# Adding x off TensorE for 14 of 16 blocks of pairs, with PSUM copies shared anew and the steps reordered

## The chip, the cores and the metric

One core of a Trainium2 chip. The rounds of the experiments ran on four different chips, so kernels of different rounds are compared by their ratios to before, which ran in every round. The metric is device time in microseconds (us), the median of several executions; lower is better. The span that the profile shows (first to last instruction) is some 2 us shorter than that time. Executions have states: a few are slow (over 1.5% above the fastest of the same kernel) and are left out of ratios.

## The reference

Linear attention over 8 batches x 8 heads x 576 rows x 64, then a highway layer (512 wide) on its 4608 rows. H and T are the carry and the gate of the kernel.

```python
q_s = softmax(q, axis=-1); k_s = softmax(k, axis=2)         # written out in the reference
kv  = einsum('bhsd,bhse->bhde', k_s, v)
x   = einsum('bhsd,bhde->bhse', q_s, kv)  -> rows of 512
H = maximum(x @ w_h, 0); T = sigmoid(x @ w_t + b_t)
out = T * H + (1 - T) * x
```

## The kernel before

Everything is written as small steps, and one list, `order`, says in which order they are issued. Each engine works off its own part of that list strictly in order. So the list is the schedule. The steps that matter here:

```python
ld = pool("ld", 3)                       # three buffers each for q, k and v in float32
def load(b, which, parts=1): ...         # nc.sync.dma_start, one batch of q, k or v
def cast_v(b, a):                        # GpSimd: half a batch of v to float16
    nc.gpsimd.tensor_copy(o, i)
def q_scale_p(b, n0, n1):                # GpSimd: exp(q) times 1/sum
    nc.gpsimd.tensor_mul(e, e, r.broadcast_to(list(e.shape)))
turned = (6, 7)
def q_turn(b, n0, n1):                   # batches 6 and 7: q is transposed by DMA, queue of SyncE
    nc.sync.dma_start_transpose(out=qsD[b][...], in_=eq[b][:, n0:n1]...)

added = lambda g: ((0, 1), (0, 1, 2), (0, 1, 2), (0, 1, 2, 3))[g]   # g: pair of batches
def add_x(c, ob):                        # blended part g += x, off TensorE
    eng = nc.vector if (c, ob) == (B - 1, 3) else nc.gpsimd
    eng.tensor_add(gv(ob), gv(ob), xv(ob))
def turn_block(t, k_, xs, us):           # output: transpose by a matmul with the identity
    if xs is not None:
        mm(dst, xs, ident, True, False)  # x added in PSUM: one 128x128 matmul more
    mm(dst, us, ident, xs is None, True)
def out_copy(g, n, eng): ...             # output tile PSUM -> SBUF on ScalarE or VectorE; every 4th: store

order = [
    # ... cut: 470 steps; here only what goes to GpSimd and SyncE near the end, in order
    ("load", 7, "k"), ("q_scale_p", 6, 4, 9), ("q_turn", 6, 0, 4), ("cast_v", 6, 0),
    ("q_turn", 6, 4, 9), ("load", 7, "v"), ("cast_v", 6, 1), ("add_x", 4, 0), ...
    ("q_scale_p", 7, 0, 4), ("add_x", 5, 0), ("q_scale_p", 7, 4, 9),
    ("cast_v", 7, 1), ("cast_v", 7, 0), ("add_x", 5, 2), ("add_x", 5, 1), ...
]   # the two queues are each in true order; how they interleave is simplified
for name, *args in order:
    steps[name](*args)
```

A *unit* is a gate or a carry of one batch and one output block (128 of the 512 columns): four 128x512 matmuls. The *k-v product* of a batch is exp(k) times v, and x of a batch is its scaled q times that. A *scaling* is one call of `q_scale_p`; each batch has two. A *filler* is a clock-keeping matmul.

The softmax here doesn't subtract the row's maximum and nothing guards it: scores larger than these inputs give would overflow.

## Time and profile before

| before | value |
|---|---|
| time, median of 3 (range) | 125.06 us (124.79 to 125.07) |
| span of the profiled run, granted clock | 122.5 us, 0.999 |
| busy: PE, VectorE, ScalarE, GpSimd | 111.3, 95.9, 92.9, 79.8 us |
| first gate; x of batches 1, 3, 6, 7 | 21.8; 29.65, 53.05, 85.06, 95.18 us |
| last matmul needed, end | 118.35, 122.53 us |

TensorE's busy time is modelled and holds clock-keeping matmuls ("warm"), so 91% is not 91% of useful work. Better signposts are the moments at which x of a batch starts: each needs q, k and v of that batch through all engines. The prediction below shows the slices, the stretches and TensorE's waits of this kernel.

### The profile page before, as it was taken

The page shows a single profiled execution, that of the slowest core. Times are in us where ns is not written, and L with a number is a line of the kernel's source. Part 1 is how long each engine was busy: PE and PEld are TensorE (multiplying, and loading weights), DVE is VectorE, ACT ScalarE, POOL GpSimd, SP SyncE. Part 2 cuts the span into 40 slices and gives each one's busy share as a digit, 9 for nine tenths or more (in the row PEclk, how much of TensorE's full clock was granted, in tenths as well). Part 3 has the DMA queues.
Part 4 walks back from the last instruction along what each step waited for, and adds up shares of the span by engine and source line. Part 5 has one row for each costly group of instructions (what it writes and reads, how often), then busy time and mean ns, then how long its engine had stood idle before and what let it go on. Part 6 is the DMA issues. An engine that isn't in the chain of part 4 may idle for free.

```text
span 122.5 us, 3361 instructions
## 1 busy us (share of the span) xinstructions
PE 111.3 (91%) x1371; PEld 61.5 (50%) x1371; DVE 95.9 (78%) x179; ACT 92.9 (76%) x130; POOL 79.8 (65%) x75
## 2 busy tenths in 40 slices
PE   4998985998999998999997999997999999999960
PEld 1344543354336444745745464454456545599830
DVE  1079796579999999999979996898656379779960
ACT  4193737496979998789979999983986895588650
POOL 2000487952279989599899899996995307934620
PEclk9999999999999999999999999999999999999999
DMA  3999999999999999999999999999977500539995
GB/s 100 388 402 408 409 399 397 410 412 411 406 412 409 402 411 412 415 398 416 417 356 404 411 411 401 418 212 246 438 171 214 219 0 0 206 144 390 423 384 175
DMA packets 20583, 41.24 MB, mean 337 GB/s; under 512 B 5460, under 2 KB 5976, under 8 KB 19544
## 3 DMA queue, kind: packets, MB, share of 16 engines
q1 hardware_dynamic: 20568, 41.03, 89.0%
q8 instruction: 10, 0.16, 0.5%
q14 instruction: 5, 0.04, 0.1%
HBM read 30.41 MB, written 9.44 MB: 325 GB/s over the span
## 4 chain that ended last, share of the span: by engine, by line
DMA 51%; PE 28%; ACT 5%; POOL 5%; SPq 3%; DVE 3%; issue 2%; ACTq 0%; POOLq 0%
DMA q<-in_q_dram 24%; DMA k<-in_k_dram 12%; PE ph L64 11%; DMA w32h<-in_moe_w_h_dram 9%; PE pt L64 9%; DMA qsD<-eq 6%; PE nat L64 5%; ACT eq L174 4%; SPq L94 3%; POOL eq L254 3%; POOL g L424 2%; PE px L64 1%; DVE r L224 1%; ACT xT L357 1%; PE psk L64 1%
## 5 line engine op out<-in xcount | busy, mean ns | idle before, releaser
L64 PE MATMUL pt<-xT,w16t 128*128 128x512 f16 x128 | 32.9, 380 | 0.4 <-ACT xT L361 0.3
L254 POOL TENSOR_TENSOR eq<-eq,r 128x1024 f16<-128x1024 f16 (+2 forms) x16 | 29.9, 1876 | 4.7 <-DVE r L242 1.6
L64 PE MATMUL ph<-xT,w16h 128*128 128x512 f16 x128 | 32.5, 379 | 0.4 <-DVE dd L405 0.2
L424 POOL TENSOR_TENSOR g<-g,xT 128x512 f16<-128x512 f16 x23 | 26.0, 1154 | 7.1 <-DVE g L413 4.9
L392 ACT ACTIVATE pt<-pt,bt 128x512 f32<-128x512 f32 (+1 forms) x40 | 24.8, 632 | 6.2 <-PE pt L64 5.2
L413 DVE SCALAR_TENSOR_TENSOR g<-pt,dd 128x512 f16<-128x512 f32 (+1 forms) x40 | 24.9, 632 | 4.9 <-ACT pt L392 4.3
L405 DVE SCALAR_TENSOR_TENSOR dd<-xT,ph 128x512 f16<-128x512 f16 x32 | 21.1, 677 | 6.7 <-PE ph L64 6.6
L174 ACT ACTIVATE eq<-q 128x1152 f16<-128x1152 f32 x16 | 18.3, 1168 | 7.1 <-DMA q<-in_q_dram 7.1
L185 POOL CAST v<-v 128x1152 f16<-128x1152 f32 x12 | 13.7, 1154 | 13.2 <-DMA v<-in_v_dram 12.8
L64 PEld LDWEIGHTS <-w16h 128*128 128x128 f16 x160 | 14.5, 98 | 13.2 <-issue 1.6
L64 PEld LDWEIGHTS <-w16t 128*128 128x128 f16 x160 | 14.3, 98 | 12.7 <-issue 1.1
L224 DVE TENSOR_REDUCE r<-eq 128x18 f32<-128x1152 f16 x12 | 16.0, 1345 | 6.0 <-ACT eq L174 6.0
L464 ACT COPY o<-nat 128x512 f32<-128x512 f32 x28 | 16.8, 601 | 4.4 <-PE nat L64 3.5
L174 ACT ACTIVATE ek<-k 128x1152 f16<-128x1152 f32 x16 | 18.4, 1175 | 1.6 <-DMA k<-in_k_dram 1.5
L64 PE MATMUL warm<-wide,ident 128*128 128x512 f16 x53 | 15.1, 427 | 1.8 <-DVE wide L144 1.8
L64 PE MATMUL nat<-ident,g 128*128 128x128 f16 x142 | 14.9, 219 | 0.2 <-DVE o L485 0.2
L64 PEld LDWEIGHTS <-g 128*128 128x128 f16 x144 | 11.4, 98 | 4.8 <-issue 0.5
L357 ACT CAST xT<-px 128x1024 f16<-128x1024 f32 x10 | 10.3, 1034 | 1.8 <-PE px L64 1.8
L64 PEld LDWEIGHTS <-ident 128*128 128x128 f16 x58 | 5.6, 106 | 8.4 <-issue 3.4
L69 PE MATMUL pq<-ident,eq 128*128 128x128 f16 x108 | 9.0, 219 | 0.9 <-DVE x L309 0.4
L274 DVE COPY qsT<-pq 128x1024 f16<-128x1024 f16 (+1 forms) x18 | 9.7, 542 | 0.0
L69 PEld LDWEIGHTS <-eq 128*128 128x128 f16 x108 | 7.1, 97 | 5.0 <-POOL eq L254 1.1
(53 smaller groups left out, 102.9 us busy)
## 6 DMA issues: line engine op xcount, KB each, us to landing
out_dram<-o SPq DMA_DIRECT2D x8, 1024.0 KB, 5.5
q<-in_q_dram SPq DMA_DIRECT2D x7, 1152.0 KB, 13.9
k<-in_k_dram SPq DMA_DIRECT2D x7, 1152.0 KB, 12.9
v<-in_v_dram SPq DMA_DIRECT2D x5, 1152.0 KB, 14.6
v<-in_v_dram SPq DMA_DIRECT2D x6, 576.0 KB, 11.7
q<-in_q_dram SPq DMA_DIRECT2D x2, 576.0 KB, 4.0
k<-in_k_dram SPq DMA_DIRECT2D x2, 576.0 KB, 6.7
w32h<-in_moe_w_h_dram SPq DMA_DIRECT2D x4, 256.0 KB, 9.9
```

The lines of the kernel that those rows point to most:

```text
L64: mm = lambda o, l, r, st, sp: nc.tensor.matmul(o, l, r, start=st, stop=sp, skip_group_check=True)
L69: nc.tensor.matmul(o, i, ident, is_transpose=True, start=True, stop=True, skip_group_check=True,)
L174: nc.scalar.activation(dst[b][:, :, 2 * a : 2 * a + 2, :], in32[which][b][:, 2 * a : 2 * a + 2].rearrange("p c n d -> p n c d"), AF.Exp,)
L185: nc.gpsimd.tensor_copy(o, i)
L224: nc.vector.reduce_sum(qsum[b][:, :, h], eq[b][:, :, h, :], axis=AX.X)
L254: nc.gpsimd.tensor_mul(e, e, r.broadcast_to(list(e.shape)))
L357: copy[how](dst, t.rearrange("p c (n d) -> p c n d", d=64))
L392: nc.scalar.activation(ps, ps, AF.Tanh, bias=bt2[:, ob : ob + 1], scale=0.5)
L405: nc.vector.scalar_tensor_tensor(dd, xv(ob), -0.5, ps, op0=ALU.mult, op1=ALU.max)
L413: nc.vector.scalar_tensor_tensor(gv(ob), th, 1.0, dd, op0=ALU.add, op1=ALU.mult)
L424: eng.tensor_add(gv(ob), gv(ob), xv(ob))
L464: copy(rows_of_four((g, n // 4))[:, n % 4, :], nat.pop((g, n)))
```

## The change

The intent is to take work off TensorE, which is full to the end. Of 16 (pair, block) combinations x is added off TensorE in 14 instead of 12; five adds go to VectorE (four of 128x512 and one of 128x256), the others to GpSimd. Copies out of PSUM are shared anew between ScalarE and VectorE. And the whole list of steps was made again, which is the largest part of the diff.

```diff
-    added = lambda g: ((0, 1), (0, 1, 2), (0, 1, 2), (0, 1, 2, 3))[g]
+    added = lambda g: ((1, 2, 3), (0, 1, 2, 3), (0, 1, 2, 3), (1, 2, 3))[g]
-    def add_x(c, ob):
-        eng = nc.vector if (c, ob) == (B - 1, 3) else nc.gpsimd
-        eng.tensor_add(gv(ob), gv(ob), xv(ob))
+    def add_x(c, ob, eng="P"):
+        by[eng].tensor_add(gv(ob), gv(ob), xv(ob))
-    def x9_copy(b, t, c=slice(0, 2)):            # also x9_done, x_left_copy: engine now given
-        nc.vector.tensor_copy(x9v[:, c, :, b, :], t)
+    def x9_copy(b, t, eng, c=slice(0, 2)):
+        copy_by[eng](x9v[:, c, :, b, :], t)
 # ... order: 559 steps replaced by 557. In the new list SyncE's queue has, near the end,
+    ("q_turn", 6, 0, 4), ("q_turn", 6, 4, 9), ("load", 7, "k"), ("load", 7, "v"), store,
+    ("q_turn", 7, 4, 9), ("q_turn", 7, 0, 4)
 # and GpSimd's queue has
+    ("cast_v", 6, 0), ("cast_v", 6, 1), five ("add_x", ...),
+    ("q_scale_p", 7, 4, 9), ("cast_v", 7, 0), ("q_scale_p", 7, 0, 4), ("cast_v", 7, 1),
+    ("add_x", 5, 0), ("add_x", 4, 0), ("add_x", 4, 3), ("add_x", 5, 2)
```

## The prediction

> **What bounds the kernel now.** I read the page's slices first, then the busy times by stretch, then the chain of work that ended last, then TensorE's timeline.
>
> ```profile
> PE   4998985998999998999997999997999999999960
> DVE  1079796579999999999979996898656379779960
> POOL 2000487952279989599899899996995307934620
> DMA  3999999999999999999999999999977500539995
> ```
>
> One digit is 3.06 us. DMA is full to about 80 us, VectorE from about 28 to 61, GpSimd nearly so from 34 to 92, and TensorE from about 22 us to the end. The stretches say it in numbers (columns: stretch, PE, PEld, DVE, ACT, POOL busy with their instruction counts, clock, DMA share, GB/s):
>
> ```profile
> 30.00:60.00 30.00, 29.08 (x362) 15.22 (x354) 29.64 (x57) 27.58 (x36) 24.26 (x18) 1.00 1.04 410
> 60.00:85.00 25.00, 23.45 (x378) 12.82 (x377) 22.13 (x39) 22.47 (x31) 23.00 (x18) 1.00 1.05 361
> 85.00:105.00 20.00, 19.96 (x217) 10.66 (x217) 13.14 (x23) 15.66 (x23) 12.87 (x11) 1.00 0.51 173
> ```
>
> So there are three regimes. To 22 us little can be multiplied before q, k, v and the weights are there. From 30 to 85 us everything is nearly full: VectorE 29.6 of 30 us, then GpSimd 23.0 of 25. From 85 us only TensorE is full; VectorE has 6.9 us free of 20 and GpSimd 7.1. The chain of waits agrees: from 85 us it is a row of TensorE groups alone, each starting where the last ended:
>
> ```profile
> 77.49 7.51 DMA qsD<-eq
> ...
> 88.12 0.28 PE nat L64 x5
> 88.40 0.86 PE pt L64 x4
> 89.27 0.86 PE ph L64 x4
> 90.13 0.28 PE nat L64 x5
> ```
>
> A gate or carry (four 128x512 matmuls) costs 0.86 us of TensorE and an output tile of five matmuls 0.28 us. With such rates (0.86 for 64 units, 0.44 for 16 half units, 0.056 per 128x128 turn or added x, 0.72 for each k-v product, 0.4 for each half of x) I sum TensorE's real work, without clock-keeping matmuls, to 91.0 us. Of it about 2.6 us is done before the first gate at 21.8 us. As 21.8 + 88.4 = 110.2 and TensorE's last needed matmul ends near 118.4, some 8 us are waits, filler and small overheads. The timeline of TensorE shows the waits that matter after 22 us, in brackets:
>
> ```profile
> 29.65 0.63 PE L64 MATMUL px<-qsT,kvn 64*64 64x512 f16 x8 [0.55 <-DVE kvn L213]
> 65.25 0.41 PE L64 MATMUL px<-qsT,kvn 64*64 64x512 f16 x4 [0.89 <-ACT xT L357]
> 85.04 0.22 PE L64 MATMUL px_l<-qsD,kvn 64*64 64x64 f16 x2 [0.70 <-DMA qsD<-eq]
> ```
>
> Besides, starts of neighbouring groups lie 0.2 to 0.45 us too far apart about ten times between 32 and 47 us, with a filler pair there too (about 2.5 us together). All avoidable waits from 22 us to the last carry come to about 6 us. That is the most a better order of steps could win.
>
> **What the Trainium skill says.** "TensorE: Matmul & The Clock Gate", section "Wait — 56ns, not 53.3ns?", gives 55.6 ns from start to start of 128-column matmuls on a warm array. The trace agrees: the output tiles' matmuls start 0.055 to 0.06 us apart, though each is shown as 0.219 us long. The 55.6 ns is what removing one saves. "SBUF — State Buffer", section "Who interferes with whom", says that a VectorE instruction with two SBUF inputs and a GpSimd instruction that reads SBUF block each other for the whole instruction. The trace fits: the same 128x288 add took 0.42 us at 16.7 us and 1.13 us at 14.1, beside a GpSimd cast. So an add of x on VectorE costs the measured 0.42 us only if GpSimd rests, as it did in the one sample of before. "Perfetto Trace Analysis", section "Optimization Strategy", says that the most-contended engine may change between regimes; the stretches above show that here.
>
> **The change part by part.**
> TensorE: x was added off TensorE for 2+3+3+4 = 12 of the 16 blocks of pairs, and is for 3+4+4+3 = 14 now. One block is 8 matmuls of 128x128, so 16 go, times 0.056 = 0.9 us, on the path because TensorE is full. The last pair gets 8 back (0.45 us, within that net). Clock-keeping matmuls fall from 58 to 46; ten of the twelve lay before 19 us or after the end, so I count 0.2 us for the rest.
> GpSimd and VectorE: 34 adds instead of 30. GpSimd has 24 of 128x512 and 5 of 128x256 (23 and 6 before); it also takes two more head casts of v and one less weight cast: 1.15 - 0.67 + 2 x 0.75 - 0.84 = +1.1 us. VectorE gains three large adds and a small one (3 x 0.42 + 0.27), four output copies (4 x 0.68), one 128x1024 copy (estimate 1.2, from two of 0.69) and one head cast (0.7); it loses five small left copies (5 x 0.27), one of 0.42 and two weight casts (2 x 0.63): about +3.1 us. ScalarE: four output copies (4 x 0.60), a 1.03 copy and three head casts (3 x 0.67) go, three weight casts (3 x 0.63) and six small copies come: about -1.8 us. The VectorE adds fall after the step of pair 6, hence in the regime where VectorE has room; they cost the end nothing, even doubled.
> Start: k of batch 0 now follows q of batch 1, the first weight and v. At the trace's cadence (q of batch 1 at 12.3 us, v of batch 0 at 15.2: 1.18 MB per 2.9 us) its second half lands at about 17.8. Exp 1.2, products 0.5, normalising 0.6, x 0.8, copies 1.3: first carry at about 22.2, instead of the first gate at 21.8; but another 0.45 us of q transposes is done by then. Net about zero, I take +0.2. v of batch 1 lands about 29 us, and x of batch 1 comes at about 31.8 instead of 29.7, with seven units done instead of six. In return the sums of q of batch 2 are done by VectorE at about 22 to 26 us, where before it waited 2.2 us, and not in the full stretch.
> Middle: I summed each engine's work by mean durations up to x of batch 3 (at 53.0 us before). From x of batch 1 on, the new order has 18.5 us of TensorE, 19 of ScalarE, 18.4 of GpSimd and about 19 of VectorE, where VectorE had 24.5. So x of batch 3 can come at 50.5 to 52. Loads are no longer held behind the first store, which in before made the queue wait from 49.7 to 58.2; q of batch 6 then came late for an exp that stood ahead of the 0.89 us wait. GpSimd can finish scaling batch 6 some 1 to 3 us sooner, and the transposes are issued before the last two loads, not among them: the 0.70 us wait should go. Of the 6 us of waits I expect 1.7 net to go; new orders bring new waits.
> Tail: after the last gate, VectorE has blend, diff, a tile copy (0.55) and only then the last blend (0.42), while before the last blend came first. That is +0.5 us.
> Sum: -0.9 - 0.2 + 0.2 - 1.7 + 0.5 = -2.1, so 125.06 becomes 123.0 us.
>
> **The rivals.**
> (1) Only the removed matmuls count: 30 to 60 us is full on VectorE, ScalarE and GpSimd alike, and the new order has the same work in it. Then -0.9 - 0.2 + 0.5 gives about 124.5. For it: all four engines near 95% there. Against: VectorE's idle time before 30 us is used.
> (2) GpSimd becomes the bound: pairs 0 and 1 have four more adds of 1.15 us, just where GpSimd has no room (23.0 of 25). Scaling of batches 5 to 7 slips by up to 4.6 us, transposes land late, and TensorE waits at x of 6 or 7: 125 to 127. Against: GpSimd rested 4.5 us for v near 30 us, and its early adds go into such gaps.
> (3) The remade order removes most of TensorE's waits, 4 of 6 us: -0.9 - 0.2 - 4 + 0.5 gives about 120.5. For it: a remade order has all waits as its object. Against: loads still pace the first 50 us at 410 GB/s, and no order makes them faster.
> (4) x of batch 1 comes late with all its followers: +1 to 2 us. Against: TensorE still has units of batch 0 to do then.
>
> **Range and chances.** My sum stands between the first and third rivals. The surest term is the 0.9 us; the waits decide, with 1.5 us of spread, and the start with 1. A range of 121.0 to 125.2 holds the sum with either of them off. Faster by over 2% is below 122.56, only 0.4 us under my number: 0.40. Slower by over 2% needs the second rival in full: 0.05. Within 2%: 0.55.
>
> **What would show it.** In the changed profile: 16 fewer matmuls of x against the identity; TensorE's waits after 22 us at about 4 us instead of 6, without the waits of 0.89 on a copy and 0.70 on the transposes; x of batch 3 at 50.5 to 52 us; first carry near 22; from 85 us again a chain of TensorE groups; last gate to the end 0.5 us longer; adds on VectorE between 0.42 and 1.2 us. Wrong: a wait of over 1 us at x of batches 6 or 7 (second rival), x of batch 3 at 53 or later (first), or a first carry after 23.

## The result, and the profile after

The changed kernel took 125.95 us (125.57 to 125.97 in three fast runs; a fourth, at 127.55, was slow). Its ratio to before is 1.0065, 95% interval 1.0036 to 1.0094. All ratios here are the mean time of one kernel's fast runs over that of the other's of the same rounds, so not quite the ratio of the medians quoted. So it is 0.7% slower where 1.6% faster was predicted, and outside the predicted range.

The slices of the changed kernel, 3.09 us each:

```profile
PE   4999157998899999999999999999959799999920
DVE  1075997999999999999999999989947369887930
POOL 2003845657997699999999999980699255704600
PEclk9999999599999999999999999999999999999995
DMA  3999999999999999999999989999949800759971
```

Two places differ. Early, TensorE is thin in slices 5 and 6 and its clock shows a 5 in slice 8 (21.7 to 24.8 us). Late, GpSimd falls to 0 in the 28th slice (83.5 to 86.6 us), and two and four slices behind it TensorE has a 5 and a 7 where before it had nines. The same stretches as those of before (columns: stretch, PE, PEld, DVE, ACT, POOL busy, clock, DMA share, GB/s):

```profile
30.00:60.00 30.00, 29.53 (x493) 15.98 (x490) 29.70 (x53) 27.87 (x41) 27.95 (x23) 1.00 1.04 409
60.00:85.00 25.00, 25.00 (x333) 13.27 (x332) 24.27 (x44) 21.06 (x28) 23.04 (x17) 1.00 1.00 341
85.00:105.00 20.00, 17.45 (x193) 9.34 (x191) 14.30 (x25) 13.42 (x22) 12.37 (x10) 1.00 0.64 196
```

Up to 85 us TensorE is better filled than before (25.00 of 25 us against 23.45). From 85 us it has 17.45 of 20, where before it had 19.96. The chain that ended last is no longer a row of TensorE groups from 85 us on (columns: start, length, what):

```profile
77.58 10.06 DMA v<-in_v_dram
...
87.76 1.15 POOL v L185
88.91 2.09 POOL eq L254
90.99 1.28 POOL v L185
92.28 4.45 POOL g L429 x4
...
96.78 0.29 PE nat L64 x2
```

The chain says: the load of v of batch 7 landed at 87.6 us, and from there to 96.7 GpSimd worked off what stood behind the cast of that v. TensorE's timeline shows the waits (in brackets) that came of it, and a third at the end:

```profile
92.33 0.48 PE L64 MATMUL psk<-v,ek 64*64 64x65 f16 x36 [1.47 <-POOL v L185]
...
96.78 0.29 PE L64 MATMUL nat<-ident,g 128*128 128x128 f16 x2 [1.07 <-POOL g L429]
...
118.70 0.23 PE L64 MATMUL nat_l<-ident,g 128*128 128x128 f16 x1 [0.72 <-DVE g L414]
```

**The balance.** I summed TensorE's gaps from the trace: start to start of neighbouring matmuls less the time that their columns take at full rate (a quarter of it for a 64x64 matmul, of which four run at once), where over 60 ns is left; so matmuls at a low rate count as gaps too. A gap belongs to the side of 85 us on which it begins.

| us | before | after | second scaling moved (experiment 1) |
|---|---|---|---|
| TensorE's gaps, 20 to 85 us | 11.4 | 9.7 | 9.8 |
| TensorE's gaps, 85 us to the last matmul | 2.3 | 4.7 | 2.0 |
| x of batch 6 starts | 85.06 | 80.50 | 80.62 |
| x of batch 7 starts | 95.18 | 94.17 | 92.67 |
| last needed matmul ends | 118.35 | 119.04 | 116.36 |

When x of batch 6 starts, the changed kernel is 4.6 us sooner, with 2.1 us more of TensorE's work still to do (34.0 against 31.9 us, my sum), so 2.5 us ahead. From there on it has 3.2 us more of gaps (0.75 us between 80 and 85 us and the 4.7, against 2.3), and its last store ends 0.55 us later after the last matmul (4.73 against 4.18 us). 2.5 - 3.2 - 0.55 gives 1.2 us behind; the spans are 123.77 and 122.53. The gain was there, and was given back within the last third.

**Theory A, the order of a queue.** v of batch 7 comes late, and in GpSimd's queue the cast of its first half stands ahead of the second scaling of q, the second cast and four adds of x, all wanted by TensorE. **Theory B, too much work:** GpSimd has 1.8 us more of busy time (81.6 against 79.8), and being the bound it makes TensorE wait anyhow. **Theory C, the clock:** with fewer fillers early, TensorE's array slows (the 5 in the clock row), and that time is lost.

### The profile page after: what moved, and what is told of

Its sections match the earlier page's. It is cut to its first block, busy times and chain, and to the rows that moved or that the text cites.

```text
span 123.8 us, 3308 instructions
## 1 busy us (share of the span) xinstructions
PE 108.4 (88%) x1343; PEld 60.3 (49%) x1343; DVE 100.9 (81%) x181; ACT 90.8 (73%) x131; POOL 81.6 (66%) x76
## 3 DMA queue, kind: packets, MB, share of 16 engines
q1 hardware_dynamic: 20600, 41.03, 89.2%
## 4 chain that ended last, share of the span: by engine, by line
DVE 27%; PE 26%; POOL 19%; DMA 14%; ACT 4%; issue 4%; SPq 2%; DVEq 1%; POOLq 0%
PE pt L64 9%; PE ph L64 9%; POOL eq L254 8%; DMA v<-in_v_dram 8%; POOL g L429 6%; DMA q<-in_q_dram 6%; DVE dd L406 5%; POOL v L185 5%; PE nat L64 4%; DVE r L224 3%; DVE g L414 3%; DVE qsT L274 3%; ACT eq L174 3%; DVE t L235 2%; DVE t L236 2%
## 5 line engine op out<-in xcount | busy, mean ns | idle before, releaser
L64 PE MATMUL pt<-xT,w16t 128*128 128x512 f16 x128 | 32.1, 380 | 0.0
L429 POOL TENSOR_TENSOR g<-g,xT 128x512 f16<-128x512 f16 x24 | 27.3, 1155 | 5.7 <-DVE g L414 5.7
L64 PEld LDWEIGHTS <-w16h 128*128 128x128 f16 x160 | 15.1, 100 | 14.3 <-issue 2.5
L468 ACT COPY o<-nat 128x512 f32<-128x512 f32 x24 | 13.8, 591 | 10.9 <-PE nat L64 8.8
L185 POOL CAST v<-v 128x1152 f16<-128x1152 f32 x12 | 14.6, 1239 | 5.3 <-DMA v<-in_v_dram 5.2
L64 PE MATMUL nat<-ident,g 128*128 128x128 f16 x142 | 13.4, 219 | 1.1 <-POOL g L429 1.1
L64 PEld LDWEIGHTS <-g 128*128 128x128 f16 x144 | 10.0, 98 | 6.0 <-POOL g L429 1.2
L64 PE MATMUL warm<-wide,ident 128*128 128x512 f16 x41 | 11.9, 444 | 0.0
L64 PE MATMUL psk<-v,ek 64*64 64x65 f16 x576 | 6.8, 194 | 3.0 <-DVE qsT L274 1.5
L358 ACT CAST xT<-px 128x1024 f16<-128x1024 f32 x9 | 9.1, 1015 | 0.0
## 6 DMA issues: line engine op xcount, KB each, us to landing
v<-in_v_dram SPq DMA_DIRECT2D x4, 288.0 KB, 11.4
```

The source lines that it names most:

```text
L64: mm = lambda o, l, r, st, sp: nc.tensor.matmul(o, l, r, start=st, stop=sp, skip_group_check=True)
L429: by[eng].tensor_add(gv(ob), gv(ob), xv(ob))
L468: copy_by[eng](rows_of_four((g, n // 4))[:, n % 4, :], nat.pop((g, n)))
```

## The experiments

Twelve kernels ran, all correct. Each was timed in five rounds against before (medians 125.0 to 125.4 us in their rounds). In the diffs, steps are moved within the list.

**1. The second scaling of batch 7 ahead of the first cast** (A against B: the same work, two neighbours in GpSimd's queue swapped).

```diff
-  ("q_scale_p", 7, 4, 9), ("cast_v", 7, 0), ... ("q_scale_p", 7, 0, 4), ... ("cast_v", 7, 1)
+  ("q_scale_p", 7, 4, 9), ("q_scale_p", 7, 0, 4), ("cast_v", 7, 0), ... ("cast_v", 7, 1)
```

> The changed kernel with one step moved: GpSimd scales the second part of q of batch 7 before, not after, it casts the first half of v of batch 7. No transfer and no amount of work changes. Theory A (GpSimd waited 4.65 us for v of batch 7 with work that it could have done queued behind it; TensorE's waits of 1.47 us at the k-v products of batch 7 and 1.07 us at an output tile follow from that): both waits go, 2 to 3 us less, 122.5 to 124 us, ratio to the kernel before 0.980 to 0.992. Theory B (GpSimd is simply given too much to add): the sum of its work is the same, so at most 0.5 us goes, ratio 1.002 to 1.008. Theory C (the loss is at the front, where TensorE's clock fell): no change.

Measured: 123.67 us, ratio 0.9857 (0.9803 to 0.991). GpSimd's timeline in this run:

```profile
80.68 4.18 POOL L254 TENSOR_TENSOR eq<-eq,r 128x1280 f16<-128x1280 f16 x2
87.03 2.24 POOL L185 CAST v<-v 128x1152 f16<-128x1152 f32 x2 [2.16 <-DMA v<-in_v_dram]
89.23 4.83 POOL L429 TENSOR_TENSOR g<-g,xT 128x512 f16<-128x512 f16 x4
```

v lands no more than 0.7 us sooner, but both scalings are done by 84.9 us, while GpSimd would have waited. The adds start at 89.2 instead of 92.2 us, and TensorE's two waits of 1.47 and 1.07 us are gone (gaps from 85 us: 2.0). One step moved, no work taken away, and 2.1% of time gone: A is shown and B falls as the explanation of this result. The changed kernel itself was not timed again in these rounds. Experiment 4, which differs from it in one step of the tail, was, and came to 1.0084 where the changed kernel had 1.0065; so the 2.1% is hardly a difference between chips or days.

**2. The load of v of batch 7 earlier** (A by the other end: the transfer instead of the queue).

```diff
-  ... ("load", 6, "v"), ... ("q_turn", 6, 4, 9), ... ("load", 7, "k"), ("load", 7, "v")
+  ... ("load", 6, "v"), ("load", 7, "v"), ... ("q_turn", 6, 4, 9), ... ("load", 7, "k")
```

> The changed kernel with the load of v of batch 7 issued right after the load of v of batch 6, ahead of the first store and of the two transposes of batch 6; GpSimd's order is kept. Theory A: GpSimd's wait of 4.65 us goes and with it TensorE's two waits, 2 to 3 us less; but the transposes of batch 6 now stand behind one more load of 1.18 MB (2.9 us), so x of batch 6 may wait 0 to 2 us anew: 123 to 125 us, ratio 0.983 to 0.999. Theory B: ratio 1.002 to 1.012. Theory C: no change.

Measured: 123.51 us, ratio 0.9873 (0.9828 to 0.9918). GpSimd no longer waits for v, with the old order of its queue:

```profile
81.44 2.35 POOL L254 TENSOR_TENSOR eq<-eq,r 128x1280 f16<-128x1280 f16 x1
83.71 1.16 POOL L185 CAST v<-v 128x1152 f16<-128x1152 f32 x1
84.82 1.91 POOL L254 TENSOR_TENSOR eq<-eq,r 128x1024 f16<-128x1024 f16 x1
```

So the same 2% is to be had at either end of the wait. x of batch 6 came at 81.3 us instead of 80.5, but that is no cost of the earlier load: x of batch 1, long before it, was already 0.8 us late in this profile (33.64 against 32.84), and from there to x of batch 6 both take 47.7 us. Why v was late is read from SyncE's queue. First the changed kernel, then before (start, length, what; a DMA is issued only when the one ahead of it has been):

```profile
73.11 3.67 SPq L283 DMA_TRANSPOSE qsD<-eq  x2
76.83 0.70 SPq L94 DMA_DIRECT2D k<-in_k_dram  x1
77.58 0.53 SPq L94 DMA_DIRECT2D v<-in_v_dram  x1
```

```profile
74.01 7.58 SPq L283 DMA_TRANSPOSE qsD<-eq  x2
81.65 0.57 SPq L94 DMA_DIRECT2D v<-in_v_dram  x1
```

In before that load was issued 4 us *later*, yet took 6.0 us from issue to landing instead of 10.06: in the changed kernel k of the same batch goes just ahead (it landed 6.2 us after its issue, and v 4.6 us after k), while before that k had been loaded ahead of the transposes. So v landed at about 87.7 us in both kernels. It hurt in one only: before, GpSimd did both scalings of batch 7 ahead of the casts. The lateness of v is not what the change brought; its place in GpSimd's queue is.

**3. Clock-keeping matmuls back** (C).

```diff
+  ("warm_up", 5), ("q_trans", 0, 1, "q2"), ... ("warm_up", 4), ("q_trans", 0, 0), ...
+  ("warm_up", 6), ("kv_half", 0, 0)
```

> The changed kernel with 15 clock-keeping matmuls added in TensorE's waits between 12 and 19 us. Theory C (the fall of the granted clock to 0.66 in the stretch 20 to 25 us costs the time): about 1 to 1.5 us less, ratio 0.995 to 0.999. Theory A: the granted clock goes back to 1 there and the first carries take half as long, but VectorE paces the stretch from 21 to 58 us, so the time changes by less than 0.4 us, ratio 1.003 to 1.009.

Measured: 124.21 us, ratio 0.9935 (0.9892 to 0.9978). The time fell, but the profile does not show it come from the early clock. In the changed kernel the first four matmuls of the first carry start 0.43 us apart and those of this one 0.21 to 0.22 us (after the first); yet x of batch 1 starts at 32.84 and 32.97 us, and every x up to batch 6 agrees within 0.15 us. What the slow array loses at 23 us is taken up by a wait that follows (in experiment 1, at full rate there, 1.7 us at 26.7 us). The profiles of experiments 1 and 4, with the same early steps as the changed kernel, say the same: their 3.4 us at half rate begin at 14.9 and 20.1 us, those of the changed kernel at 21.2, and x of batch 1 starts within 0.1 us of 32.8 in all three. Only in experiment 2 did it last 6.8 us (from 14.5), and there x of batch 1 was 0.8 us late; that the clock was the cause was not tested. The profile's gain comes later: the two transposes held SyncE's queue 2.94 us instead of 3.67, v landed at 86.5 instead of 87.6 us, and TensorE's wait of 1.47 us at the last k-v product is gone while that at the output tile (1.24 us) stays. So in this profile it is A again. Why fillers near 15 us should bring v sooner isn't shown, and it may be chance: in experiment 4, without these fillers, that load was issued at the same moment (76.98 us against 77.02), and its v was cast from 87.92 us instead of 86.64. The 1.3% that this kernel's six runs gained over the changed one thus has no shown cause.

**4. The tail.** VectorE's copy of the second-last output piece after the last blend.

```diff
-  ("tile9_copy", 2, 3, "V"), ("blend", 9, 3)
+  ("blend", 9, 3), ("tile9_copy", 2, 3, "V")
```

> The changed kernel with the last blend on VectorE moved ahead of the copy of the last but one tile. The wait of 0.72 us before the last matmuls should shrink to 0.3 to 0.4, and the end should come 0.2 to 0.4 us sooner: ratio 1.002 to 1.006. If the last stores and not VectorE set the end, no change.

Measured: 126.55 us, ratio 1.0084 (1.0017 to 1.015; two of six runs slow), no gain that the timing resolves. In the profile TensorE's gap ahead of its last matmuls went from 0.88 to 0.64 us, so the order of the tail is worth 0.24 us.

**5. Experiments 1 and 3 together.**

> The changed kernel with both mends: GpSimd scales the second part of q of batch 7 before it casts v of batch 7, and 15 clock-keeping matmuls stand in TensorE's early waits. If the two losses are separate (theory A plus C), the gains add: scale7_first gave 0.9857, keep_warm 0.9935, the change itself 1.0065, so 0.9857 x 0.9935 / 1.0065 = 0.973, about 121.9 us. If keep_warm gained only because v of batch 7 happened to land 1.1 us sooner in its profile, nothing is added: 0.983 to 0.988. The granted clock of all runs should be at or above 0.99 and the spread of the runs under 1.5 us if the fall of the clock made the spread.

Measured: 122.87 us, ratio 0.9781 (0.9726 to 0.9836), the best of all: 2.2% faster than before. Its profiled run counts as slow and started everything 1.9 us late, but from x of batch 0 to x of batch 7 it takes 71.4 us, as experiment 1 does (71.6; the changed kernel 73.1, before 76.0 with another split of the work). The intervals of experiments 1 and 5 overlap, so what the fillers add beyond the moved step, some 0.8% by the means, isn't settled. The sign set for the clock (all runs at 0.99 or above, spread under 1.5 us) did not show: the clocks are 0.981 to 0.998, the spread 2.4 us. The following kernels start from this one, but 8 (from before) and 11 (from experiment 1).

**6. Five adds from VectorE to GpSimd** (is the sharing of the adds needed, and does GpSimd's load matter?).

```diff
-  ("add_x", 5, 3, "V"), ("add_x", 5, 1, "V"), ("add_x", 4, 1, "V"), ("add_x", 6, 3, "V"), ("add_x", 8, 1, "V")
+  the same with "P", at the same places
```

> As the kernel 'both', with the five adds of x that VectorE does given to GpSimd. If they are on VectorE for a reason: GpSimd has four times 1.15 us and once 0.67 more between 84 and 112 us, the output tiles of pairs 2 and 3 wait for it, 0.5 to 2.5 us more than 'both'. If VectorE's adds are neutral, as the prediction said (they lie where it has room, and so does GpSimd after 97 us): within 0.4 us of 'both'.

Measured: 126.77 us; only two of the six runs were fast (124.51 and 125.27), and by them the ratio is 0.9969 (0.9894 to 1.0045) against 0.9781. In the profile, itself of a slow run (126.6 us), the seven adds in a row hold TensorE:

```profile
89.14 7.79 POOL L429 TENSOR_TENSOR g<-g,xT 128x512 f16<-128x512 f16 x7
```

```profile
96.99 0.28 PE L64 MATMUL nat<-ident,g 128*128 128x128 f16 x2 [1.98 <-POOL g L429]
```

So GpSimd is no bound in the changed kernel, but has little room: three adds more, 3 us, and TensorE waits 2 us. In this profile a second loss stands behind that wait: the granted clock is 0.50 from 98.3 to 101.7 us. The two fast runs had a mean clock of 1.0, the four slow ones 0.95 to 0.976. By those two fast runs the adds on VectorE are worth some 2%.

**7. Twelve blocks instead of fourteen, in the best order** (what are the removed matmuls worth?).

```diff
-  added: (1, 2, 3), (0, 1, 2, 3), (0, 1, 2, 3), (1, 2, 3)
+  added: (2, 3), (1, 2, 3), (0, 1, 2, 3), (1, 2, 3)      # and the four add_x of these blocks left out
```

> As the kernel 'both', with x of one block of pair 0 and one of pair 1 added on TensorE again (16 matmuls more, four adds of 1.15 us less on GpSimd): 12 of 16 blocks as in the kernel before. If TensorE is the bound of the whole, 16 x 0.056 = 0.9 us more. If GpSimd paces the stretch from 59 to 97 us, its 4.6 us less work there lets x of batches 6 and 7 come sooner, and the time is the same or up to 1.5 us less. If VectorE paces it, no change from GpSimd and 0 to 0.9 us more from TensorE's end.

Measured: 124.47 us, ratio 0.9939 (0.989 to 0.9987). The mean span of the fast runs rose from 120.8 to 121.8 us, 1.0 us for 16 matmuls; at 0.056 us each they make 0.9. (The mean time of the fast runs rose by 1.9 us; what is over lies outside the span and is not explained.) By the span, the removed matmuls are worth what the rate says, with four adds on GpSimd as their price.

**8. Fourteen blocks in the old order** (does the diff's first line alone help?). Adds of (0, 2), (1, 2), (2, 3) and (3, 3) set behind their blends, all on GpSimd; all else as before.

> The kernel before with one part of the change alone: x added on GpSimd for two more blocks (block 2 of pair 0, block 3 of pair 1), 14 of 16, in the order of before; copies and VectorE's adds as before. If only the removed matmuls counted: 0.9 us less, ratio 0.993. With GpSimd full from 35 to 76 us in that order, its four adds of 1.15 us put off the scaling of batches 5 and 6 by up to 4.6 us and the transposes with them: TensorE's wait at x of batch 6 grows from 0.9 to 2 to 4 us, ratio 1.005 to 1.025.

Measured: 126.34 us, ratio 1.0088 (1.0039 to 1.0137). TensorE now waits where before it did not, and for the transposes a little longer (0.81 instead of 0.70 us):

```profile
71.19 0.48 PE L64 MATMUL psk<-v,ek 64*64 64x65 f16 x36 [0.73 <-ACT ek L174]
...
77.33 0.23 PE L64 MATMUL nat<-ident,g 128*128 128x128 f16 x1 [0.60 <-POOL g L424]
...
86.53 0.22 PE L64 MATMUL px_l<-qsD,kvn 64*64 64x64 f16 x2 [0.81 <-DMA qsD<-eq]
```

Earlier there are two more for GpSimd, 0.69 us at 47.61 (a scaling) and 0.38 us at 48.72 (an add); x of batch 3 came at 53.9 us instead of 53.05. The wait at x of batch 6, expected to grow to 2 to 4 us, did not. Here theory B holds, as far as these waits tell: at the places chosen, the old order had too little room on GpSimd for 4.6 us of adds, and 0.9 us saved on TensorE became 1.1 us lost. Other places in the old order were not tried.

**9. Six output copies from VectorE back to ScalarE** (is the sharing of copies needed?).

```diff
-  ("out_copy", 0, 1, "V"), (0, 2), (0, 5), (0, 7), (1, 1), (1, 2) likewise
+  ("out_copy", 0, 1, "A"), ...
```

> As the kernel 'both', with the six copies of output tiles of pairs 0 and 1 that VectorE does given back to ScalarE (6 x 0.68 us less on VectorE, 6 x 0.59 more on ScalarE, all between 55 and 85 us). If VectorE paces that stretch (it is busy 24 of 25 us from 60 to 85, ScalarE 21), x of batch 6 comes 0.5 to 2 us sooner. If GpSimd paces it (24.9 of 25), x of batch 6 stays where it is, and the time is within 0.5 us of 'both'. If sharing the copies was right, ScalarE's exps and copies of x come later and the time is 0.5 to 2 us longer.

Measured: 125.6 us, ratio 1.0016 (0.9967 to 1.0065) against 0.9781. In the stretch from 63 to 95 us (columns as above), first the best version (its slow profile, 1.1 us later at the first x), then this one:

```profile
63.00:95.00 32.00, 32.00 (x449) 17.13 (x448) 30.81 (x54) 26.78 (x37) 30.63 (x23) 1.00 0.96 321
```

```profile
63.00:95.00 32.00, 30.89 (x437) 16.84 (x436) 26.59 (x46) 27.88 (x40) 28.32 (x21) 1.00 1.01 311
```

VectorE gets 4.2 us freer, ScalarE busier by only 1.1, and TensorE has new waits for what ScalarE copies: 0.23 us at 65.8, 0.40 at 75.5 and 0.31 at 87.8 in its timeline; from x of batch 4 to x of batch 7 it took 32.0 us instead of 30.4. ScalarE is not full by its busy share (27.88 of 32 us); its copies simply come late in its queue. This sharing was right, and worth 2.4% by the two ratios.

**10. Later sums for batch 2, a cast moved to ScalarE** (does VectorE's full stretch at 21 to 34 us cost the end?).

```diff
-  ("q_sums_tree", 2, 1) and ("q_recip", 2) ahead of ("diff", 0, 2); ("cast_v_head", 1, 2, "V")
+  both behind ("diff", 0, 0); ("cast_v_head", 1, 2, "A") behind ("exp_half", 1, "k", 1)
```

> As the kernel 'both', with VectorE's sums of the second half of q of batch 2 (1.2 us) after its first three diffs instead of before, and one cast of v of batch 1 (0.74 us) on ScalarE. If VectorE's order paces the start, TensorE's wait of 0.5 to 1.6 us before the fourth carry goes and x of batch 1 comes 0.3 to 0.9 us sooner, and the time falls by 0.3 to 0.9. If loads pace it (v of batch 1 lands near 29 us), x of batch 1 moves by under 0.3 and the time by under 0.3.

Measured: 123.77 us, ratio 0.9862 (0.9819 to 0.9905) against 0.9781, no gain. The wait was moved on, not removed. TensorE's wait near 30 us in the best version, then its successor here:

```profile
30.24 1.02 PE L64 MATMUL ph<-xT,w16h 128*128 128x512 f16 x4 [1.47 <-DVE dd L406]
```

```profile
33.06 0.27 PE L69 MATMUL pq<-ident,eq 128*128 128x128 f16 x2 [1.55 <-DVE qsT L274]
```

VectorE hardly rests there in either (busy 9.86 and 9.78 us of the 10 from 23 to 33 us), so what is put off holds the next thing.

**11. No clock-keeping matmuls at all** (C, from the other side; based on experiment 1).

> As scale7_first (ratio 0.9857), with no clock-keeping matmuls at all[...]. If the clock at the front does not set the time (VectorE and the loads pace it), x of batches 1 and 3 stay within 0.3 us and the time within 0.5 us of scale7_first. If it does (theory C), the first carries and the k-v products at half clock put x of batch 1 off by 1 us or more, ratio 0.992 or above, and the runs spread as the clock comes back sooner or later.

Measured: 124.3 us, ratio 0.993 (0.9888 to 0.9972) against 0.9857 for experiment 1. Turns of q start 106 to 107 ns apart up to 22.4 us, where a warm array has 55 to 56. The loss by the means is 0.7%; the intervals just overlap. The profiled run was slow, so I don't read the loss from it. By these numbers all fillers together are worth about 0.7%, and that they are worth anything is only just shown. The ratio is the one that theory C expected (0.992 or above), so C is not refuted: beside the wait that A explains, a loss by the clock of some 1% stays possible, in experiments 3, 5 and 11 alike.

**12. The best version with the earlier load of v too** (are the cures of experiments 1 and 2 the same?).

> The best version so far (first scaling of batch 7 ahead of its cast of v, fillers kept) with the load of v of batch 7 also moved up behind the load of v of batch 6. Both single edits took TensorE's waits at the last k-v product and at the output tile behind it away. Theory: they cure one and the same wait, so together they give no more than one: ratio to the kernel before 0.974 to 0.986 (0.978 without this edit), GpSimd's wait for v gone, but x of batch 6 later by about 0.7 us as it was with the moved load alone (81.3 against 80.5). Rival: the two edits take away different waits and their gains add: ratio under 0.972, with x of batch 7 at least 0.7 us sooner after the first x than in the best version (71.4 us).

Measured: 123.01 us, ratio 0.9835 (0.9775 to 0.9895), no better than without. From the first x to x of batch 7 it takes 71.5 us (71.4 without), and to x of batch 6 59.5 (59.4), so the 0.7 us that the earlier load was expected to cost there did not come. The two cures take away one and the same wait.

## Why the prediction was wrong, point by point

**The failed step: the waits, "-1.7".** Until 85 us this term had the right sign: TensorE's gaps fell from 11.4 to 9.7 us. That this is just 1.7 is luck, since it hangs on the gap at x of batch 6 of before, 0.9 us, which ends at 85.04 us and is counted on this side. The waits of 0.89 and 0.70 us that it named went. What failed is the path behind the sentence "the transposes are issued before the last two loads, not among them: the 0.70 us wait should go". The sentence came true, but it looked only at when transfers are issued and at the wait that this removes. The prediction did not follow the last v to its landing, nor ask what stood behind its cast in GpSimd's queue. New waits of 1.47 and 1.07 us came (gaps from 85 us: 2.3 to 4.7). Over the whole run the term was +0.7 instead of -1.7. Experiment 1 takes those waits away by one moved step and is 1.4% faster than before, 1.8 us, near the 2.1 us of the sum.

**The rivals.** One reading behind them was wrong: "all four engines near 95%" in 30 to 60 us. The prediction's own line has GpSimd at 24.26 of 30 us, 81%; there it had room for adds, and after the change it has 27.95. The first (only the matmuls count, 124.5) was wrong as a mechanism, as waits did change much, in both directions. The second named the right engine and sign (GpSimd, TensorE waiting late, 125 to 127), but another cause, too much work from the added x. That cause is real in the old order (experiment 8) and with three adds more in a row (experiment 6), but not in the changed kernel, where GpSimd rested 4.65 us at that very point. My sign "a wait of over 1 us at x of batches 6 or 7" was too narrow: the waits came at the k-v product of batch 7 and the output tile. The third (120.5) asked for more than any order here gave; the best, 122.9, is close to the sum itself (123.0), but with a step moved and 15 fillers put back, so it does not confirm it. The fourth was wrong: x of batch 1 did come 3.2 us later, but not its followers (see the start, below).

**The 16 matmuls, "-0.9".** Right by the span: 1.0 us in experiment 7 (1.9 us by the time).

**The filler, "-0.2".** Its sign is doubtful: putting 15 fillers back made the kernel 1.3% faster, though its profile shows only an earlier v, and taking all away made it 0.7% slower (experiment 11). Open.

**The start, "+0.2".** Too small, and without cost. The first carry came at 22.9 instead of 22.2 us, at half rate, and x of batch 1 at 32.8 instead of 31.8. By x of batch 2 the changed kernel was 1.0 us sooner than before (40.1 against 41.1).

**The middle.** x of batch 3 came at 52.5 us (53.05 before; I had 50.5 to 52, and 53 or later as the refutation): the right way, but 0.5 us where 1 to 2.5 were expected. x of batch 6 was 4.6 us sooner.

**VectorE's adds, "cost the end nothing, even doubled".** They did not hold the end, but "nothing" undersold them: without them the kernel loses 2% (experiment 6). Three of them in the changed kernel:

```profile
86.14 0.41 DVE L429 TENSOR_TENSOR g<-g,xT 128x512 f16<-128x512 f16 x1
...
88.81 0.42 DVE L429 TENSOR_TENSOR g<-g,xT 128x512 f16<-128x512 f16 x1
...
89.75 1.53 DVE L429 TENSOR_TENSOR g<-g,xT 128x512 f16<-128x512 f16 x1
```

The first had GpSimd at rest and took 0.41 us; the third had a scaling on GpSimd beside it and took 1.53. That agrees with the Trainium skill, "SBUF — State Buffer", section "Who interferes with whom", which the prediction drew on; it passed the predicted upper bound of 1.2.

**The tail, "+0.5".** Right in sign, and half the size: the order of the last steps costs 0.24 to 0.25 us (experiment 4; 1.59 against 1.34 us from the last gate to the last matmul). From the last gate to the end it was 0.8 us, but 0.55 of that is the last store, whose end lies 3.8 to 4.7 us after the last matmul in these profiles, whatever the tail's order.

## What to carry to other kernels

When a change moves a transfer or reorders an in-order queue, follow the latest operand to its landing and list what stands behind its first user: work that is ready belongs ahead of work that waits, and one swapped pair was worth 2% here. A gain in the middle counts only if the last stretch can take it up, so compare how far each kernel is at several fixed points (which batch, how much work left), not busy shares. And parts of one change can need each other: the adds alone lost 0.9% in the old order, and gained in the new one.

## What the Trainium skill lacked or had wrong

- "TensorE: Matmul & The Clock Gate", "Part 1: The HAM clock gate (the "warmup" mystery)", says that the array falls to half rate after an idle window of about 3.4 us. The rates agree (106 to 107 and 55 to 56 ns per 128 columns), but in the changed kernel the granted clock was halved from 21.2 to 24.7 us with no wait above 1.5 us in the ten us before. In the two stretches of 3.4 us before it TensorE was busy 1.70 and 2.05 us; in experiment 6's profile 1.42 of the 3.4 us before 98.3. So a partly busy stretch did not keep the clock up in these two cases.
- No page that I found gives a time for which a DMA transpose holds the queue that issues it on this chip ("DMA: Bandwidth & Descriptors" has cycle counts for trn3 and for unnamed earlier generations): the two of batch 6, issued with their inputs ready, held it 2.8 to 4.5 us in the kernels of the new order (3.67 in the changed one), and those of batch 7 in the changed kernel 9.1 us, as the second's input was not ready, with the store behind them not issued.
- "SBUF — State Buffer", "Who interferes with whom", gives the lock, not its size: a VectorE add of 128x512 took 0.41 us alone and 1.53 us beside a GpSimd multiplication of 2.13 us.
